# A fused attention-and-MLP kernel: the order of loads, LayerNorm steps and first projections in its head

## The chip, the cores and the metric

The kernel runs on one core of one Trainium2 chip. The metric is device time in microseconds (us) of one execution, lower is better. TensorE multiplies matrices, VectorE (DVE) and ScalarE (ACT) work on elements and empty the accumulators, GpSimd (POOL) works on elements in SBUF, and SyncE (SP) issues most transfers. ACT issues some transfers too, on a DMA queue of its own.

## What is computed

```python
xn = layernorm(x)                                   # x: 2048 x 448, bf16
qkv = xn @ wqkv                                     # 448 x 1344, 16 heads of 28
pq, pk = q @ w_phi[h], k @ w_phi[h]                 # per head 28 x 28
phi = concat(softmax(p), softmax(-p))               # for q and for k: 56 features a head
kv, z = phi_k^T @ v, sum(phi_k)                     # per head 56 x 28, and 56
o = (phi_q @ kv) / (phi_q @ z + 1e-6)
out = x + o @ wo + silu(xn @ w1) @ w2               # w1: 448 x 1792, w2: 1792 x 448
```

All sums over the sequence are linear, so `kv` and `z` are accumulated over all 2048 rows first, and the outputs are made in a last phase.

## The kernel before

**Tiling.** The 2048 rows are 16 tiles of 128 rows (`t`), in four chunks of four tiles (`c`). The depth of 448 is seven slices of 64 rows (`s`). Operands lie twice, in partitions 0 to 63 (LO) and 64 to 127 (HI), and matmuls are issued in pairs (`pair`, L420; all matmuls carry L429, all transposes by TensorE L442), one on each half of the array. Three double banks of PSUM, the slots, are handed round by `take` and `give`; a slot can be written again when its last content has been copied out.

**The units of work.** `LN_a` and `LN_b` (L529 to L548) make the LayerNorm of one tile: on DVE statistics (`bn_stats`, L532, 128x448), `bn_aggr` (L533), the variance plus epsilon (L535, on DVE for tiles 0 and 1, else on POOL), on POOL the power -0.5 (L537), and on DVE the normalised tile `xnd` (L547). Tiles 0 to 3 are transposed by TensorE (`X_tr`), and `X_ev` (L570) copies the two halves to `xT`, one with ACT (L447) and one with DVE (L579). Tiles 4 to 15 are transposed by DMA (`X_dma`, L559). `F1` is `xn @ w1` for one `i` of seven (128 columns of each half of `w1`) and two or four tiles, followed by Silu on ACT into `hT`; `F1p` is the same for one tile and two `i`. `FT_tr` transposes the q and k part of `wqkv`, and its four or three results are copied out by ACT and DVE (L768); `FM` multiplies them with the block-diagonal `BD` of `w_phi` into `wqk`, and each of the four FM results is copied out half by ACT and half by DVE (L788). `QK` is `xn @ wqk` for a tile, with two Exp on ACT, sums on DVE (L620), a reciprocal (L622) and two products on POOL (L627). `V` is `xn @ wv` for two tiles. `F2_early` is `hT @ w2` for one tile (28 matmuls). `KV` accumulates `kv` and `z`.

**What sets the order.** The program is recorded as a list of operations with dependencies, and a planner (`_Prog.schedule`, L199) decides the order on each engine. TensorE's operations stay in the order in which they are written down. Operations with `ordered=True` keep their written order among themselves on their engine; all loads are ordered. The others are sorted by the planner with costs that stand in the code; a transfer is taken to cost `nbytes / 280` ns after those before it (L300). Each engine then works strictly in its planned order and waits on semaphores.

**The head.** The loads are issued on SP as: x tile 0, x tile 1, `w1` part 0 and part 1, x tiles 2-3, `w1` part 2 and 3, wqk (two loads), `w_phi` (four small loads into `BD`), x tiles 4-7, `wv` (two loads), then `w2` in two loads, each after a mark in TensorE's order. `w1` has four parts of 256, 256, 256 and 128 columns; each part is a low load on SP (L493) and a high load on ACT's queue (L494). TensorE's order is: 36 warm-up pairs; `X_tr` of tile 0; 3 warm-up pairs; `X_tr` of tile 1; 3 warm-up pairs; `F1p` of tile 0 and of tile 1; `F1` for `i` 2 to 6 of tiles 0 and 1, with `X_tr` of tiles 2 and 3 between; `F1` for all seven `i` of tiles 2 and 3 with `FT_tr` (two) and `FM` 0 and 1 between; then `phase_e(0)` (L851): V(0), FM(2), F2_early(0) with FM(3) in its middle, QK(0), QK(1), F2_early(1), QK(2), QK(3), V(2). After that the four-tile `F1` of chunk 1 begins.

DVE's order in the head (what the planner made of it) is: statistics of tiles 0 and 1, `xnd` of tile 0 and the first part of tile 1, the copy of tile 0, the rest of `xnd` of tile 1, **`bn_stats` of tile 2, then the copy of tile 1**, the rest of tiles 2 and 3, their copies, and then `bn_stats` of tile 4 ahead of the first `FT_tr` copies.

Of the kernel before, what the change touches and what calls it, by code (L numbers as in the profile page):

```python
# [138 lines left out]
class _Prog:  # L139
# [89 lines left out]
    def _pass(self, when):  # L229
        ops = self.ops  # L230
        n = len(ops)
        lat = self.lat
        tend = max(when.values()) + 3000.0
        for o in reversed(ops):
            if o.eng == "pe":
                o.alap = when[o.id]
                continue
            m = tend
            for u in o.users:
                uu = ops[u]  # L240
                if u in o.odeps:
                    continue
                m = min(m, uu.alap - (lat(o, uu) if o.id in uu.deps else 0.0))
            extra = 0.0
            if o.is_dma:
                extra = o.fixed if o.fixed is not None else 2000.0 + o.nbytes / 280.0
            o.alap = m - o.dur - extra
# [24 lines left out]
        while done < n:  # L272
            best = None
            for e in ENGINES:
                if not ready[e]:
                    continue
                c = [(est(ops[i]), ops[i]) for i in ready[e]]
                t0 = min(x[0] for x in c)
                t, o = min(((t, o) for t, o in c if t <= t0 + WAIT_TOL), key=lambda x: (x[1].alap, x[1].id))
                for t2, o2 in c:  # L280
                    if o2 is o or o2.alap >= o.alap or t2 >= t + o.dur:
                        continue
                    la = max(t - o.alap, t + o.dur - o2.alap, 0.0)
                    lb = max(t2 - o2.alap, t2 + o2.dur - o.alap, 0.0)
                    if lb < la - 1.0:
                        t, o = t2, o2
                if best is None or t < best[0]:
                    best = (t, o)
            assert best is not None, "scheduler deadlock"
            t, o = best  # L290
            ready[o.eng].discard(o.id)
            o.start = t
            if o.is_dma:
                issue_end = t + o.dur
                eng_free[o.eng] = issue_end
                if o.fixed is not None:
                    o.end = t + o.fixed
                else:
                    x0 = max(issue_end + 900.0, dma_free[0])
                    dma_free[0] = x0 + o.nbytes / 280.0  # L300
                    o.end = dma_free[0] + 300.0
            else:
                o.end = t + o.dur
                eng_free[o.eng] = o.end + (0.0 if o.eng == "pe" else 30.0)
                if o.eng == "act" and o.table is not None:
                    act_table[0] = o.table
            order[o.eng].append(o.id)
            done += 1
            for u in o.users:
                ndeps[u] -= 1  # L310
                if ndeps[u] == 0:
                    ready[ops[u].eng].add(u)
# [3 lines left out]
def bass_parallel_sum__linear_kernel_hedgehog__dense_activation_silu__prompt_kernel(  # L316
# [16 lines left out]
    NB = 4  # L333
# [4 lines left out]
    with es:  # L338
# [117 lines left out]
        def load(dst, src, nbytes, name, eng="sp", issue=650.0, after=None):  # L456
            return P.dma(lambda e: e.dma_start(out=dst, in_=src), nbytes, writes=[dst], name=name, eng=eng,  # L457
                         issue=issue, ordered=True, after=after)
# [5 lines left out]
        pool(lambda e: e.memset(neghalf[:], -0.5), 110, [], [neghalf[:]], "neghalf")  # L464
        pool(lambda e: e.memset(ones_bf[:], 1.0), 230, [], [ones_bf[:]], "ones")
        pool(lambda e: e.affine_select(ident[:], ones_bf[:], [[1, 128]], ALU.is_equal, 0.0, base=0,
                                       channel_multiplier=-1), 290, [ones_bf[:]], [ident[:]], "ident")
# [16 lines left out]
        def load_x(t0, t1, after=None):  # L484
            load(x_sb[:, t0:t1, :], xv[:, t0:t1, :], (t1 - t0) * 128 * D * 2, f"x{t0}", issue=430, after=after)

        w1v = B_w1.rearrange("(s p) f -> p s f", p=64)
        W1S = [0, 256, 512, 768, 896]

        def load_w1(i):  # L490
            a, b = W1S[i], W1S[i + 1]
            n = D * (b - a) * 2
            load(w1_sb[LO, :, a:b], w1v[:, :, a:b], n, f"w1l{i}")  # L493
            load(w1_sb[HI, :, a:b], w1v[:, :, 896 + a:896 + b], n, f"w1h{i}", eng="act")  # L494
# [3 lines left out]
        load_w1(0)  # L498
        load_w1(1)
        load_x(2, 4)  # L500
        load_w1(2)
        load_w1(3)
        load(wraw[:, 0:3, 8:904], A_wqkv[0:384, 0:896].rearrange("(b p) c -> p b c", p=128), 384 * 896 * 2, "wqk0")
        load(wraw[LO, 3, 8:904], A_wqkv[384:448, 0:896], 64 * 896 * 2, "wqk1")
        pool(lambda e: e.memset(BD[:], 0.0), 300, [], [BD[:]], "bd0")
        for p0 in (0, 904):
            pool(lambda e, p0=p0: e.memset(wraw[:, :, p0:p0 + 8], 0.0), 150, [], [wraw[:, :, p0:p0 + 8]], "wpad")
        wpv = A_w_phi.rearrange("(k q l) d f -> q l d k f", q=2, l=2)
        for q in range(2):
            for l in range(2):  # L510
                p0 = (64 if q else 8) + l * DH
                load(BD[p0:p0 + DH, :, l * DH:(l + 1) * DH], wpv[q, l], DH * NB * DH * 2, f"wphi{q}{l}", issue=430)
        wvv = A_wqkv[:, 2 * D:3 * D].rearrange("(s p) c -> p s c", p=64)
        load_x(4, 8)
        load(wv_sb[LO], wvv, D * D * 2, "wv0")
        load(wv_sb[HI], wvv, D * D * 2, "wv1")
# [4 lines left out]
        for sl in range(NE):  # L521
            pads = E[:, sl].rearrange("p k (c n) -> p (k c) n", n=64)[:, :, 56:64]
            pool(lambda e, pads=pads: e.memset(pads, 0.0), 330, [], [pads], "pads")
        for sl in range(NV):
            onesc = vb[:, sl].rearrange("p t (h c) -> p (t h) c", c=DH + 1)[:, :, DH:DH + 1]
            pool(lambda e, onesc=onesc: e.memset(onesc, 1.0), 150, [], [onesc], "vones")


        def LN_a(t, od=False):  # L529
            P.unit = f"LN{t}"  # L530
            xs = x_sb[:, t, :]
            P.op("dve", 630, lambda e: e.bn_stats(st6[:, t, :], xs), [xs], [st6[:, t, :]], name="bnst", ordered=od)  # L532
            P.op("dve", 180, lambda e: e.bn_aggr(mv[:, t, :], st6[:, t, :]), [st6[:, t, :]], [mv[:, t, :]], name="bnag", ordered=od)  # L533
            P.op("dve" if od else "pool", 90 if od else 220,
# [15 lines left out]
        def LN(t):  # L550
            LN_a(t)
            LN_b(t)
# [17 lines left out]
        def X_ev(t, sl, od=False):  # L570
            P.unit = f"X{t}"
            j = t % 4
            for q in range(2):
# [19 lines left out]
        def F1p(t, i):  # L593
            P.unit = f"F1p_{t}_{i}"
            sl = take()
            for u in range(2):
                for s in range(NS):
                    pair([(bank(2 * sl + q)[:, u * 128:(u + 1) * 128], w1_sb[HALF[q], s, (i + u) * 128:(i + u + 1) * 128],
                           xT[HALF[q], 0, s, t * 128:(t + 1) * 128], s == 0, s == NS - 1) for q in range(2)], 128, "f1")
            src = two(sl)[:, :, 0:256].rearrange("p b (u n) -> p b u n", u=2)  # L600
# [30 lines left out]
        def V(t):  # L631
# [3 lines left out]
            for s in range(NS):  # L635
                pair([(bank(2 * sl + q)[:, 0:D], xT[HALF[q], c % NXC, s, (j + q) * 128:(j + q + 1) * 128], wv_sb[HALF[q], s, :],
                       s == 0, s == NS - 1) for q in range(2)], D, "v")
            dstv = vb[:, (t // 2) % NV].rearrange("p t (h c) -> p t h c", c=DH + 1)[:, :, :, 0:DH]
# [88 lines left out]
        def WO(t, ub, sl):  # L727
# [19 lines left out]
            P.dma(lambda e: e.dma_start(out=ov[:, t:t + 2, :], in_=x_sb[:, t:t + 2, :]), 2 * 128 * D * 2,  # L747
# [45 lines left out]
        LN_a(0, True)  # L793
        LN_a(1, True)
        PARTS = ((0, HS), (HS, NS))
        LN_b(0, PARTS, True)
# [5 lines left out]
        X_ev(0, s0, True)  # L802
        LN_b(1, PARTS[1:], True)
        P.unit = "warm"
        warm(3)
        X_tr(1, s1, 0, HS)
        X_tr(1, s1, HS, NS)
        X_ev(1, s1, True)
        P.unit = "warm"
        warm(3)  # L810
        give(s0)
        F1p(0, 0)
        give(s1)
        F1p(1, 0)
        for t in (2, 3):
            LN_a(t)
            LN_b(t)
        marks = []
        for i in range(2, FH):
            F1(0, i, 0, 2)  # L820
            marks.append(P.ops[P.last[("pe", "o")]])
            if i in (3, 5):
                t = 2 + (i - 3) // 2
                sl = take()
                X_tr(t, sl, 0, NS)
                X_ev(t, sl)
                give(sl)
        for i in range(FH):
            F1(0, i, 2, 2)
            marks.append(P.ops[P.last[("pe", "o")]])  # L830
            if i in (0, 2):
                FT_tr(i // 2)
            if i in (4, 6):
                FM((i - 4) // 2)
        load(w2_sb[:, 0:7], w2v[:, 0:7], FF * D, "w2", after=marks[5])
        load(w2_sb[:, 7:14], w2v[:, 7:14], FF * D, "w2", after=marks[6])

# [13 lines left out]
        def phase_e(c, f2):  # L851
            t = 4 * c
            if c == 0:
                V(0)
                FM(2)
                F2_early(f2[0], lambda: FM(3))
                QK(0)
                mk = P.ops[P.last[("pe", "o")]]
                load_x(8, 12, after=mk)
                load_x(12, 16, after=mk)  # L860
                QK(1)
                F2_early(f2[1])
                QK(2)
                QK(3)
                V(2)
# [4 lines left out]
            if c == 1:  # L870
                for s in range(NS):
                    for q in range(2):
                        load(wo_sb[HALF[q], s, :], wov[s], 64 * D * 2, f"wo{s}", after=mk)
# [148 lines left out]
```

## Time and profile before

| | us |
|---|---|
| median of 6 runs (157.48 to 158.63) | 157.72 |
| the profiled execution | 157.05 |
| its span, first to last instruction | 155.3 |
| TensorE busy | 145.7 (94%) |
| DVE / ACT / POOL busy | 93.9 / 93.4 / 84.0 |
| mean granted TensorE clock | 0.989 |
| start of the first V matmuls | 25.05 |
| start of the first QK matmuls | 30.03 |
| start of chunk 1's `F1` matmuls | 39.30 |

Times in the profile count from the span's first instruction. In the timeline a line gives the start, the length from the first to the last instruction of a merged group, the engine, the source line, the operation, output and input, the count, and in brackets how long the engine had been idle and who ended it. The waits list sums such idle time. The chain of waits follows what ended last back to the start. The stretches give busy time of each engine with the number of instructions, the granted clock, the DMA engines' busy share and GB/s. "To landing" is the time from the start of a transfer's issue to its last byte's report.

### The profile page before, as it was taken

What the parts mean: (1) busy time and instruction counts of PE and PEld (TensorE: products, weight loads), DVE (VectorE), ACT (ScalarE), POOL (GpSimd) and SP (SyncE); (2) the same over time, 40 slices, a digit from 0 to 9 for tenths busy, and PEclk for the clock granted to TensorE, in tenths of its full rate; (3) what the DMA queues carried; (4) which work ended last, traced back from release to release, by engine and by line L of the source; (5) the groups of instructions that cost most, each with busy time, mean ns of one, the idle gap of its engine ahead of it and who ended that gap; (6) DMA issues with size and microseconds to landing.
All of it is one profiled execution on the core that took longest, in us unless ns stands there. A gap on an engine that the chain in (4) does not pass through costs nothing.

```text
span 155.3 us, 5241 instructions
## 1 busy us (share of the span) xinstructions
PE 145.7 (94%) x2290; PEld 95.5 (61%) x2290; DVE 93.9 (60%) x170; ACT 93.4 (60%) x120; POOL 84.0 (54%) x97
## 2 busy tenths in 40 slices
PE   5829998999999999999999999999999999999990
PEld 5729887666556666555666666666556666666650
DVE  2744197639996667990129797862046464946652
ACT  3215788597995977795689577588563324033330
POOL 6412007022899995969902999977993311222220
PEclk9995999999999999999999999999999999999999
DMA  4999987783030895397883022523170020111203
GB/s 120 236 241 299 174 257 207 125 195 124 0 72 4 160 181 121 93 90 148 163 153 59 4 68 68 72 68 72 41 166 2 4 103 19 63 59 56 72 0 118
DMA packets 38639, 16.60 MB, mean 107 GB/s; under 512 B 30104, under 2 KB 38232, under 8 KB 38616
## 3 DMA queue, kind: packets, MB, share of 16 engines
q1 hardware_dynamic: 36760, 15.47, 45.7%
q10 hardware_dynamic: 1856, 0.80, 2.4%
q8 instruction: 18, 0.29, 0.9%
q14 instruction: 5, 0.04, 0.1%
HBM read 7.48 MB, written 1.84 MB: 60 GB/s over the span
## 4 chain that ended last, share of the span: by engine, by line
PE 89%; DMA 4%; SPq 1%; DVE 1%; issue 1%; ACT 1%; DVEq 0%
PE psum L429 87%; DMA x_sb<-in_A_x_dram 4%; PE psum L442 2%; SPq L457 1%; DVE st L532 0%; DVE x_sb L743 0%; ACT hT L447 0%; DVEq L973 0%; ACT xT L447 0%; DVE xT L579 0%; DVE mv L533 0%
## 5 line engine op out<-in xcount | busy, mean ns | idle before, releaser
L627 POOL TENSOR_TENSOR E<-E,Rk 128x896 bf16<-128x896 bf16 x32 | 53.2, 1697 | 10.1 <-DVE Rk L622 8.3
L429 PE MATMUL psum<-xT,w_sb 64*128 64x512 bf16 (+2 forms) x518 | 48.0, 332 | 2.9 <-DVE mv L533 2.7
L429 PE MATMUL psum<-w_sb,hT 64*128 64x448 bf16 x448 | 45.4, 349 | 0.0
L447 ACT ACTIVATE hT<-psum 128x1024 bf16<-128x1024 f32 (+1 forms) x35 | 29.2, 853 | 13.9 <-PE psum L429 13.2
L429 PEld LDWEIGHTS psum<-xT,w_sb 64*128 64x128 bf16 x518 | 27.3, 97 | 16.0 <-issue 2.9
L620 DVE TENSOR_REDUCE Sk<-E 128x64 f32<-128x1792 bf16 x16 | 31.9, 2003 | 5.1 <-ACT E L447 4.9
L429 PEld LDWEIGHTS psum<-w_sb,hT 64*128 64x128 bf16 x448 | 25.2, 94 | 15.4
L447 ACT ACTIVATE E<-psum 128x896 bf16<-128x896 f32 x32 | 27.4, 917 | 6.6 <-PE psum L429 5.2
L447 ACT ACTIVATE xT<-psum 128x896 bf16<-128x896 bf16 (+2 forms) x20 | 13.0, 690 | 27.7 <-PE psum L442 25.4
L429 PE MATMUL psum<-wqk,xT 64*128 64x448 bf16 x224 | 23.7, 349 | 0.0
L689 POOL TENSOR_TENSOR xT<-xT,x_sb 128x448 f32<-128x448 f32 x8 | 8.3, 1034 | 25.1 <-ACT xT L447 22.4
L429 PEld LDWEIGHTS psum<-wqk,xT 64*128 64x128 bf16 x224 | 13.0, 94 | 7.8
L547 DVE TENSOR_SCALAR xnd<-x_sb,mv,rstd 128x896 bf16<-128x896 bf16 (+2 forms) x18 | 11.5, 666 | 8.7 <-POOL rstd L537 8.6
L677 POOL TENSOR_TENSOR Ye<-Ye,x_sb 128x448 f32<-128x448 f32 x8 | 8.2, 1031 | 12.9 <-DVE Ye L675 12.9
L532 DVE BATCH_NORM_STATS2 st<-x_sb 128x6 f32<-128x448 bf16 x16 | 9.4, 606 | 7.8 <-DMA x_sb<-in_A_x_dram 7.8
L429 PE MATMUL psum<-wv_sb,xT 64*128 64x448 bf16 x112 | 12.1, 349 | 0.0
L429 PE MATMUL psum<-wo_sb,xT 64*128 64x448 bf16 x112 | 11.9, 349 | 0.0
L535 POOL TENSOR_SCALAR ve<-mv 128x1 f32<-128x1 f32 x14 | 2.8, 216 | 15.9 <-DVE mv L533 15.9
L675 DVE TENSOR_TENSOR Ye<-psum,Ye 128x448 f32<-128x448 f32 x8 | 5.0, 621 | 9.2 <-ACT Ye L447 6.0
L714 DVE TENSOR_TENSOR xT<-psum,rden 128x224 bf16<-128x224 f32 x32 | 10.2, 381 | 0.2
L537 POOL TENSOR_TENSOR rstd<-ve,neghalf 128x1 f32<-128x1 f32 x16 | 8.9, 565 | 1.7 <-DVE ve L535 1.0
L743 DVE TENSOR_TENSOR x_sb<-psum,Ye 128x448 bf16<-128x448 f32 x8 | 4.6, 619 | 7.7 <-PE psum L429 7.7
(45 smaller groups left out, 112.5 us busy)
## 6 DMA issues: line engine op xcount, KB each, us to landing
out_dram<-x_sb SPq DMA_DIRECT2D x8, 224.0 KB, 1.9
w_sb<-in_B_w_dram SPq DMA_DIRECT2D x2, 784.0 KB, 5.5
x_sb<-in_A_x_dram SPq DMA_DIRECT2D x3, 448.0 KB, 4.4
wv_sb<-in_A_wqkv_dram SPq DMA_DIRECT2D x2, 392.0 KB, 10.2
wo_sb<-in_A_wo_dram SPq DMA_DIRECT2D x14, 56.0 KB, 2.2
w_sb<-in_B_w_dram ACTq DMA_DIRECT2D x3, 224.0 KB, 5.2
w_sb<-in_B_w_dram SPq DMA_DIRECT2D x3, 224.0 KB, 6.1
phT<-in_A_wqkv_dram SPq DMA_DIRECT2D x1, 672.0 KB, 10.8
```

What stands on the lines that cost most here:

```text
L429: ins = e.matmul(dst, lhsT, rhs, start=st, stop=sp, skip_group_check=True)
L447: return P.op("act", d_act(n), lambda e: e.activation(dst, src, func, scale=scale), reads=reads or [src], writes=writes or [dst], table=ta ...
L532: P.op("dve", 630, lambda e: e.bn_stats(st6[:, t, :], xs), [xs], [st6[:, t, :]], name="bnst", ordered=od)
L537: P.op("pool", 580, lambda e: e.tensor_tensor(rstd[:, t:t + 1], ve[:, t:t + 1], neghalf[:], ALU.pow), [ve[:, t:t + 1], neghalf[:]], [rstd[ ...
L547: lambda e, dst=dst, src=src: e.tensor_scalar(dst, src, mv[:, t, 0:1], rstd[:, t:t + 1], ALU.subtract, ALU.mult),
L620: dve(lambda e: e.tensor_reduce(Sk[:, t % 3, :].rearrange("p (h g) -> p h g", g=2), Er, AXL.X, ALU.add), d_dve(1792), [Er], [Sk[:, t % 3, ...
L627: pool(lambda e, Eh=Eh, Rb=Rb: e.tensor_tensor(Eh, Eh, Rb, ALU.mult), 1770, [Eh, Rh], [Eh], "phi%d" % qk)
L675: dve(lambda e: e.tensor_tensor(y, b, y, ALU.add), d_dve(D), [b, y], [y], "ye_d")
L677: pool(lambda e: e.tensor_tensor(y, y, x_sb[:, t, :], ALU.add), 1110, [y, x_sb[:, t, :]], [y], "ye_x")
L689: pool(lambda e: e.tensor_tensor(y, y, x_sb[:, t, :], ALU.add), 1110, [y, x_sb[:, t, :]], [y], "yl_x")
L714: dve(lambda e, dst=dst, src=src, rb=rb: e.tensor_tensor(dst, src, rb, ALU.mult), d_dve(224), [src, r], [dst], "o")
L743: dve(lambda e, b=b, y=y, dst=dst: e.tensor_tensor(dst, b, y, ALU.add), d_dve(D), [b, y], [dst], "out")
```

## The change

It does the following.

- The loads: `w1` comes in three parts of 256, 256 and 384 columns. x tiles 2-3 are issued after `w1` part 0 instead of after part 1. The four `w_phi` loads go to ACT's queue, after its three `w1` loads. x tiles 4-7 become two loads of two tiles, no longer ahead of `wv`: SP's order after wqk is `wv`, x 4-5 (after the mark of `F1` i=3, tiles 0-1), the first half of `w2` (after i=5), x 6-7 (after i=5), the second half of `w2` (after i=6). The loads of x tiles 8-15 stand ahead of the four transposing DMAs of tiles 4-7 on SP; before they stood behind them.
- POOL: the constants and the clearing of `BD` and of the pads of `wqk`'s raw tile are ordered, the first constants ahead of `BD`; the nine other memsets (`pads`, `vones`) come after the powers of tile 3.
- DVE and POOL run tiles 0 to 3 in a written order. `bn_stats` of tile 2 still stands ahead of the copy of tile 1. The epsilon step of tiles 2 and 3 goes from POOL to DVE.
- TensorE: ten warm-up pairs stand after `X_tr` of tile 0 (instead of three and three); `X_tr` of tile 1 comes in the middle of `F1p` of tile 0; `X_tr` of tile 3 and the `FT_tr` and `FM` steps move by one `F1` or two; `phase_e(0)` is V(0) with FM(2) inside, V(2) with FM(3) inside, QK(0), QK(1), F2_early(0), QK(2), QK(3), F2_early(1).
- The planner's cost of a transfer is `nbytes / run * (12 + 0.0475 * run) / 16` ns, with `run` the bytes of one contiguous piece. With it the planner puts all four DVE copies of the `FT_tr` results together; then come `bn_stats` of tiles 4 and 5, the copies of FM(0) and FM(1), `bn_stats` of tile 6, the copy of FM(2), `bn_stats` of tile 7, the copy of FM(3), and then the four `bn_aggr` and the four `xnd` of tiles 4 to 7. Before, the four `xnd` stood between the copies of FM, and all four `bn_stats` ahead of them.

From chunk 1's `F1` on, the order of TensorE's units is the same as before.

```diff
-        W1S = [0, 256, 512, 768, 896]
+        W1S = [0, 256, 512, 896]
...
         load_w1(0)
+        load_x(2, 4)
         load_w1(1)
-        load_x(2, 4)
         load_w1(2)
-        load_w1(3)
...
-                load(BD[...], wpv[q, l], DH * NB * DH * 2, f"wphi{q}{l}", issue=430)
+                load(BD[...], wpv[q, l], DH * NB * DH * 2, DH * 2, f"wphi{q}{l}", eng="act", issue=430)
...
-        load_x(4, 8)
...
-        LN_a(0, True)
-        LN_a(1, True)
         PARTS = ((0, HS), (HS, NS))
+        LN_st(0, True)
+        LN_ag(0, True)
+        LN_st(1, True)
+        LN_ag(1, True)
...
-        X_ev(0, s0, True)
+        X_ev(0, s0, (0, 1), True)
         LN_b(1, PARTS[1:], True)
+        LN_st(2, True)
         P.unit = "warm"
-        warm(3)
-        X_tr(1, s1, 0, HS)
-        X_tr(1, s1, HS, NS)
-        X_ev(1, s1, True)
-        P.unit = "warm"
-        warm(3)
+        warm(10)
         give(s0)
-        F1p(0, 0)
+
+        def x1():
+            X_tr(1, s1, 0, HS)
+            X_tr(1, s1, HS, NS)
+            X_ev(1, s1, (0, 1), True)
+            LN_ag(2, True)
+            LN_st(3, True)
+            LN_ag(3, True)
+            LN_b(2, od=True)
+            LN_b(3, od=True)
+            pads_init()
+
+        F1p(0, 0, x1)
         give(s1)
         F1p(1, 0)
-        for t in (2, 3):
-            LN_a(t)
-            LN_b(t)
...
-            if i in (3, 5):
+            if i in (3, 4):
...
-            if i in (0, 2):
+            if i in (1, 3):
                 FT_tr(i // 2)
-            if i in (4, 6):
-                FM((i - 4) // 2)
-        load(w2_sb[:, 0:7], w2v[:, 0:7], FF * D, "w2", after=marks[5])
-        load(w2_sb[:, 7:14], w2v[:, 7:14], FF * D, "w2", after=marks[6])
+            if i in (5, 6):
+                FM(i - 5)
+        load_x(4, 6, after=marks[1])
+        load(w2_sb[:, 0:7], w2v[:, 0:7], FF * D, 896, "w2", after=marks[3])
+        load_x(6, 8, after=marks[3])
+        load(w2_sb[:, 7:14], w2v[:, 7:14], FF * D, 896, "w2", after=marks[4])
...
-                V(0)
-                FM(2)
-                F2_early(f2[0], lambda: FM(3))
+                V(0, lambda: FM(2))
+                V(2, lambda: FM(3))
                 QK(0)
                 mk = P.ops[P.last[("pe", "o")]]
+                QK(1)
+                F2_early(f2[0])
                 load_x(8, 12, after=mk)
                 load_x(12, 16, after=mk)
-                QK(1)
-                F2_early(f2[1])
                 QK(2)
                 QK(3)
-                V(2)
+                F2_early(f2[1])
```

`LN_st` and `LN_ag` are the first and the other steps of `LN_a`; `F1p` and `V` call what they are given after the first of their two halves and after their third slice.

## The prediction, made before the result was known

> **What bounds the kernel now.** I read the waits of TensorE first, then the chain, then the timeline of the head, then the stretches with the clock. The chain ends in one TensorE piece without a gap:
>
> ```profile
> 3.15 6.59 DMA x_sb<-in_A_x_dram
> ...
> 9.76 0.63 DVE st L532
> 10.39 0.29 DVE xT L579
> ...
> 10.83 3.78 PE psum L429 x56
> ...
> 27.13 87.45 PE psum L429 x1114
> ```
>
> From 27.13 to 114.58 nothing but TensorE is on the path, and little else to the end. So the change can win only before 27.13, and whatever it wins there moves the end one for one, as long as TensorE finds its operands at chunk 1 (39.30 now). TensorE's waits up to there:
>
> ```profile
> PE psum L429 <- DVE mv L533: 2.7, 1, 2.7
> PE psum L429 <- POOL ident L466: 1.7, 1, 1.7
> PE psum L429 <- issue: 0.5, 1, 0.5
> PE psum L442 <- DVE xnd L547: 0.4, 1, 0.4
> ```
>
> The longest one is named after DVE's L533, but DVE's timeline shows what it is:
>
> ```profile
> 9.76 0.63 DVE L532 BATCH_NORM_STATS2 st<-x_sb 128x6 f32<-128x448 bf16 x1 [2.94 <-DMA x_sb<-in_A_x_dram]
> 10.30 0.37 DVE L579 COPY xT<-psum 128x448 bf16<-128x448 bf16 x1
> ...
> 19.36 0.63 DVE L532 BATCH_NORM_STATS2 st<-x_sb 128x6 f32<-128x448 bf16 x1 [1.94 <-DMA x_sb<-in_A_x_dram]
> 19.91 0.74 DVE L768 COPY phT<-psum 128x512 bf16<-128x512 bf16 x2
> ```
>
> The copy of tile 1, which TensorE needs for F1p(1), stands behind bn_stats of tile 2, which waits for x 2-3. The same pattern comes again at 19.36: bn_stats of tile 4 waits for x 4-7 and holds the FT copies. The idle time also costs clock:
>
> ```profile
> 8.40:11.80 3.40, 0.97 (x32) 1.00 (x34) 1.73 (x6) 0.33 (x1) 0.86 (x3) 1.00 1.23 236
> 11.80:15.20 3.40, 3.40 (x47) 3.02 (x45) 1.63 (x3) 1.75 (x4) 0.70 (x2) 0.51 1.06 302
> ```
>
> After a stretch in which TensorE was busy 0.97 of 3.40 us the clock is 0.51 for as long: 3.4 x 0.49 = 1.7 us of work lost. DMA is at 1.06 to 1.23 throughout: the head is fed by a saturated queue.
>
> **The loads in the new order.** Issue plus time to landing gives, in us, x0 2.9, x1 3.4, w1 low parts 6.4, 8.6, 11.6, 12.3, high parts 4.9, 7.0, 10.1, 10.7, x 2-3 9.7, wqk 15.9 and 16.8, x 4-7 19.3, wv 20.1 and 21.2, w2 23.3 and 26.5. I move these steps as a queue.
>
> - x 2-3 take 1.17 (9.74 - 8.57) behind w1 part 0, no longer behind part 1: 6.4 + 1.2 = 7.6. w1 part 1 then ends where both ended before, 9.75.
> - w1's last two parts took 2.6 (9.74 to 12.34). Their 688 KB moved at about 240 GB/s with 512-byte pieces and 215 with 256-byte ones, 2.98 us; the piece of 768 bytes is not in the trace. Bounds: no gain, and 1.0 at the 359 GB/s of 12 to 13 us (1792-byte pieces). I take 0.7, nearest to the 512-byte row. The four w_phi loads now share the engines with this part: 24 KB in 448 pieces, 0 to 0.56 us if a piece costs as much as those of the transposes (800 a us at 28 us); I take 0.3. So w1 is complete at 12.34 - 0.7 + 0.3 = **11.9**.
> - wqk follows 4.5 later as now: 16.4. From there to the end of wv were 4.3, of which x 4-7 (448 KB at 255 to 310 GB/s) were 1.6: wv at 19.1. x 4-5 follow 0.8 later, 19.9; the first w2 half at 340 GB/s, 2.2; x 6-7, 0.7: **22.8**. Check: what lies ahead of and in x 6-7 is the very set that had landed at 23.25 before, with the queue nearly dry (72 GB/s) from 18.4 to 20.4.
>
> The DMA page of the Trainium skill (DMA: Bandwidth & Descriptors, section Queues, rings and completion order) says that an engine takes turns between the queues by packet, which speaks against putting w_phi beside w1's last part; an estimate by it would delay that part by up to w_phi's whole time. No row separates the two.
>
> **TensorE step by step.** F1p(1) starts 1.09 after x 2-3 land now (9.74 to 10.83: bn_stats 0.63, copy 0.37). New: 7.6 + 1.1 = 8.7, **instead of 10.83**. Ahead of it all fits: ten warm-up pairs are 0.5 (three are 0.16), ending near 6.5, when ACT's copy of tile 0 (5.96 + 0.54) ends too. F1p(1) ends at 9.5, F1(2) waits for w1 part 1 to 9.8, two F1 (0.77 each; 28 matmuls took 1.54) and X_tr(2) (0.2) end at 11.55, and F1(4) waits for w1's last part: 11.9. So half of what x 2-3 win is lost to w1, a queue that the move doesn't shorten.
>
> From 11.9: ten F1 7.7, X_tr 0.2, two FT 0.92, two FM 0.44 give V(0) at 21.2; three of its seven pairs (0.57), FM(2) 0.22, the rest 0.76, three pairs of V(2) 0.57: FM(3) at 23.3. Its slot was FM(2)'s, whose DVE copy now stands behind bn_stats of tile 6: 22.8 + 0.63 + 0.62 (L788) + 0.1 = 24.15, a **new wait of 0.85**. (At FM(0) the same pattern with x 4-5 at 19.9 costs 0.5, which the later wait swallows.) Queued behind FM(3) are V(2)'s rest and QK(0): 24.15 + 0.15 + 0.76 = 25.05. Four QK and two F2 (1.325 and 2.65 each) end at 35.65, where chunk 1's F1 starts, **instead of 39.30: 3.65 less**. In this I let no clock drop remain, since the new idle pieces (0.9, 0.3, 0.35, 0.85) lie apart.
>
> What hides the rest: the nine POOL memsets moved (six of 0.3, three of 0.24, 2.6 in all) lie at 10.4 to 13, and POOL is next needed after x 4-7, beyond 24. The epsilon step on DVE is 0.15 instead of POOL's 0.22. The w_phi issues take 1.9 (6.33 to 8.23 on SP) and end on ACT near 5.3, 0.6 ahead of its first copy; if longer, the wait for w1 still covers a us. ident comes 0.2 earlier and moves only warm-up work. Exp starts with a table load (1.28) behind V(2)'s copy; the two Exp of QK(0) then end near 29.1, and QK(2), which wants that slot, comes at 30.4. Transposes of tiles 4 to 7 now stand behind x 8-15 on SP: issued from QK(0)'s end plus about 1.1, at 1.3 each, landing 3.0 after the last issue, some 9.4 after QK(0)'s start; if they also queue behind 896 KB at 340 to 390 GB/s, 10.2 to 10.7; needed at 10.6. I charge 0.15. Sum: 3.5 less.
>
> The Trainium skill (TensorE: Matmul & The Clock Gate, section Why this matters for your kernels) wants no idle gaps over about 3 us; here 2.74 us cost 3.4 us at half clock, so the trace is stricter. If the rule held, the drop would have another cause and could stay: the sum by it would be 1.8 less, not 3.5.
>
> **Rivals.**
>
> 1. x 6-7 land by 21.9 and the copies never wait: TensorE runs through from 11.9, QK(0) at 24.2, chunk 1 at 34.8, 4.5 less: 153.2. For: the dry queue of 18.4 to 20.4. Against: the slowest engine reported wv only at 21.2. Chance 0.20.
> 2. The clock still drops: 1.7 back, 155.9. For: 0.97 busy of 3.40 sufficed. Against: the new gaps are short. 0.09.
> 3. tiles 4 to 7 land late behind x 8-15 and F1 of chunk 1 waits about 1: 155.2. 0.08.
> 4. Slower: x 6-7 behind wv and half of w2 hold FM(2)'s copy, FM(3) and QK(0) one for one. It decides from a landing at 22.8 + 3.65 = 26.4 on; at 27.4 the kernel is 1 us slower, 158.7. For: the second half of w2 landed at 26.5, and bn_stats of tile 4 did hold FT copies. Against: the bytes. 0.06.
> 5. x 2-3 don't land earlier, since ACT's queue takes the time that part 1 leaves (at 4 to 10 us both queues were full): F1p(1) at 10.8 and all behind it as before: 157.7. 0.05.
>
> **Numbers.** The profiled execution took 157.05 (span 155.3, 1.75 around it), 0.67 below the median 157.72. 157.05 - 3.5 = 153.55; on the scale of the median **154.2**, chance 0.52. The range 152.9 to 156.2 takes in rivals 1, 2 and 3 and the landing of x 6-7 from 21.5 to 24.6. About 0.5% (0.8 us) is what a measurement can tell from no change. Faster by more: 0.52 + 0.20 + 0.09 + 0.08 = 0.89; within: 0.05; slower: 0.06.
>
> **What would show it.** x 2-3 landing near 7.6 and F1p(1) near 8.7; clock 1.00 at 9 to 16 us; F1(4) waiting for DMA to 11.9; bn_stats of tile 6 with idle time from DMA ahead of it, and TensorE waiting at FM(3); QK(0) near 25 and chunk 1's F1 near 35.7. I am wrong if TensorE's waits move to ACT, if a stretch at 0.5 stays, or if idle time comes after 39.

## The result and the profile after

The changed kernel takes **158.86 us** (median of 27 runs, 157.83 to 160.86) against 157.75 (62 runs, 156.06 to 159.18) of the kernel before: ratio 1.008, 95% interval 1.006 to 1.010. It is slower by 0.8%, where 154.2 was forecast. The profiled execution took 158.86, its span is 157.1, the mean granted clock 0.978. Ratios below are all to the kernel before, on the same chip. A ratio leaves out executions more than 1.5% above the fastest of the same kernel; this weighs most in e2 below, where six of twelve fall out and the median of all twelve, 157.12, is 0.995 of the 157.89 of before.

The chain of waits of the changed kernel (start, length, what):

```profile
1.70 6.93 DMA w_sb<-in_B_w_dram
...
10.76 4.46 PE psum L429 x48
...
15.54 0.49 issue
...
21.25 0.42 issue
...
26.64 0.42 issue
...
36.63 4.58 DMA xT<-xnd
...
41.35 18.66 PE psum L429 x236
```

Chunk 1's F1 starts at 41.35, not at 39.30 as before and not at 35.65 as forecast. Three things stand on the chain: a load of `w1` near its head (before, one of x), three stops that no semaphore explains ("issue"; before, two of 0.20 and 0.47), and, wholly new, a transposing DMA ahead of chunk 1. TensorE's waits of the same profile name the same (total, times, longest):

```profile
PE psum L429 <- issue: 1.3, 3, 0.5
PE psum L442 <- DVE xnd L554: 1.2, 1, 1.2
PE psum L429 <- DMA xT<-xnd: 1.2, 1, 1.2
PE psum L429 <- DMA w_sb<-in_B_w_dram: 1.2, 1, 1.2
```

The old wait of 2.7 on F1p(1)'s copy is gone as such, but F1p(1) starts at 10.76 (before 10.83). DVE's timeline of the changed kernel shows why:

```profile
9.79 0.63 DVE L536 BATCH_NORM_STATS2 st<-x_sb 128x6 f32<-128x448 bf16 x1 [2.03 <-DMA x_sb<-in_A_x_dram]
10.33 0.37 DVE L587 COPY xT<-psum 128x448 bf16<-128x448 bf16 x1
```

It is the old pattern at the old time: x 2-3 land at 9.77 (before 9.74), and the copy of tile 1 stands behind their statistics. Ahead of it stand two waits of 1.2, one on `xnd` (0.4 before; x 1 lands at 4.84, before 3.44) and a new one on `w1` part 0 (8.62, before 6.41).

The stretches of the changed kernel (busy time with instructions for PE, PEld, DVE, ACT and POOL, then clock, DMA share, GB/s):

```profile
8.00:11.30 3.30, 2.58 (x54) 2.33 (x56) 1.48 (x5) 1.08 (x2) 0.24 (x1) 0.50 1.20 219
11.30:14.70 3.40, 3.40 (x45) 2.78 (x43) 1.93 (x5) 1.25 (x3) 2.84 (x11) 0.50 1.10 264
```

The half clock, one stretch before, is two now. **The account:** TensorE's named waits ahead of chunk 1 sum to 5.7 before and 6.3 after (with the wait for `ident`, 1.7 and 1.4), 0.6 more. Busy time at half clock cost 3.40 x 0.49 = 1.7 before and (2.58 + 3.40) x 0.50 = 3.0 after, 1.3 more. Together 1.9 of the 2.05 by which chunk 1 came later. This adds up one execution and shows no cause, and the clock's part is not borne out by the others: of the 25 executions counted, the twelve with a mean clock of 0.973 to 0.978, like the profiled one, took 158.66 on average, and the ten with 0.985 to 0.988, so with less time at half clock, took 159.18. The experiment a3 shows why it can be so. The profiled execution before lay 0.7 below its median, so the medians differ by less, 1.1. From chunk 1's F1 to the last matmul all seventeen profiles of this study show 111.8 to 112.0: only the head matters.

### The profile page after: what moved, and what is told of

Same layout as the page of the kernel before. It is cut to its first block, busy times and chain, and to the rows that moved or that the text cites. A ratio compares the mean times of both kernels' runs of the same rounds, so it can differ in the third digit from the quotient of the medians.

```text
span 157.1 us, 5256 instructions
## 1 busy us (share of the span) xinstructions
PE 147.0 (94%) x2298; PEld 93.6 (60%) x2298; DVE 94.0 (60%) x172; ACT 93.6 (60%) x120; POOL 83.7 (53%) x95
## 4 chain that ended last, share of the span: by engine, by line
PE 88%; DMA 7%; issue 1%; DVE 1%; SPq 1%; DVEq 0%
PE psum L429 86%; DMA w_sb<-in_B_w_dram 4%; DMA xT<-xnd 3%; PE psum L442 2%; SPq L460 1%; DVE Ye L687 0%; DVE x_sb L755 0%; DVEq L990 0%; SPq L567 0%
## 5 line engine op out<-in xcount | busy, mean ns | idle before, releaser
L429 PE MATMUL psum<-xT,w_sb 64*128 64x512 bf16 (+2 forms) x518 | 49.5, 340 | 3.4 <-DMA xT<-xnd 1.2
L429 PEld LDWEIGHTS psum<-w_sb,hT 64*128 64x128 bf16 x448 | 24.6, 94 | 16.5
L429 PEld LDWEIGHTS psum<-wqk,xT 64*128 64x128 bf16 x224 | 12.1, 94 | 8.6
L429 PE MATMUL psum<-wo_sb,xT 64*128 64x448 bf16 x112 | 11.9, 349 | 0.0
```

The source lines that it names most:

```text
L429: ins = e.matmul(dst, lhsT, rhs, start=st, stop=sp, skip_group_check=True)
```

## The experiments

The theories: ScalarE's queue, which starts 0.21 earlier in the changed kernel (first `w1` load at 0.93 instead of 1.14), delays x 1 and `w1` part 0 (in expectations A); the loads of x 8-15 ahead of the transposes delay chunk 1 (B); `w_phi` on ScalarE's queue slows the last part of `w1` (C); the wait and the half clock at F1p(1) are on the path (D); TensorE stops where its next block of instructions has not been fetched (F); a wait taken away at F1p(1) comes back at a later copy behind later statistics (E).

**a1_act_later: ScalarE's loads 0.21 later** (the changed kernel with `BD`'s memset ahead of POOL's constants, which shifts these loads back to 1.14).

```diff
+        P.op("pool", 300, lambda e: e.memset(BD[:], 0.0), [], [BD[:]], name="bd0", ordered=True)
...
-        P.op("pool", 300, lambda e: e.memset(BD[:], 0.0), [], [BD[:]], name="bd0", ordered=True)
```

> The changed kernel with one edit: POOL clears BD ahead of the first constant again, so that ACT's first load is issued some 0.2 us later, at about 1.14 as before the change (0.93 now). Theory A (the early start of ACT's queue puts w1's high parts ahead of x 1 and of w1's low part): x 1 lands near 3.5 instead of 4.84, w1's low part 0 near 6.5 to 7 instead of 8.62, x 2-3 near 8 instead of 9.77, the first F1p starts near 7.2; the total goes down by 0.3 to 1, the rest being held by w1's last part (13.85). Rival (the two queues share the engines by chance): landings within 0.5 of the changed kernel's, total the same.

Measured: 158.41, ratio 1.0024 (0.9999 to 1.005). x 1 lands at 3.99 (changed kernel 4.84), `w1` part 0 at 6.74 (8.62), F1p(0) starts at 7.00 (8.67), F1p(1) at 10.04. Five profiles with the early start show x 1 at 4.8 or later and F1p(0) at 7.8 to 9.3; those with the late start have F1p(0) at 6.9 to 7.4. That start is a cause, shown. But x 2-3 come at 8.95 even so, not at 7.6, and of 1.7 us gained at F1p(0) only 0.6 reach chunk 1 (40.74): two stops of 1.19 and 1.25 without a named cause follow, and the wait ahead of chunk 1 is 1.5.

**a2_x8_late: x 8-15 behind the transposes** (the changed kernel; the mark of these loads goes from QK(0) to QK(2)).

```diff
                 QK(0)
-                mk = P.ops[P.last[("pe", "o")]]
                 QK(1)
                 F2_early(f2[0])
+                QK(2)
+                mk = P.ops[P.last[("pe", "o")]]
                 load_x(8, 12, after=mk)
                 load_x(12, 16, after=mk)
-                QK(2)
```

> The changed kernel with one edit: the loads of x 8-15 take their mark from QK(2) instead of QK(0), which puts them behind the four transposing DMAs of tiles 4-7 on SP, as they stood before the change. Theory B (the transposes wait behind 896 KB on the queue and chunk 1's F1 waits for them): the wait of 1.2 us ahead of chunk 1's F1 (start 41.35) goes, F1 starts near 40.0, total 1.2 to 1.4 less than the changed kernel, 157.5, level with before. Rival (the transposes are late since their xnd are late, which stay behind all FM copies on DVE): the last transpose lands at 40 to 41 still, total within 0.5 of the changed kernel.

Measured: 157.78, ratio 1.0004 (0.997 to 1.0037), 1.2 us less than the changed kernel. Its chain runs into chunk 1 without a DMA:

```profile
29.92 10.21 PE psum L429 x108
40.13 0.06 issue
40.20 4.91 PE psum L429 x43
```

Chunk 1 starts at 40.20 instead of 41.35: the whole wait of 1.2. In all five profiles with x 8-15 ahead of the transposes this wait is there, 0.5 to 1.5; in the six with them behind it is 0.3 once (f2) and else nothing.

**a3_wphi_sp: `w_phi` back on SP, behind wqk** (the changed kernel).

```diff
-                load(BD[...], wpv[q, l], ..., eng="act", issue=430)
+                load(BD[...], wpv[q, l], ..., eng="sp", issue=430)
```

> The changed kernel with one edit: the four w_phi loads go back to SP's queue, behind wqk. Theory C (their 448 small pieces on ACT's queue slow w1's last low part): that part lands at 12.5 to 13 instead of 13.85, wqk and wv follow some 0.5 to 1 earlier, total 0.3 to 1 less. Rival (the part is late because everything ahead of it is): it lands within 0.5 of 13.85, total the same.

Measured: 158.58, ratio 1.0041 (1.0009 to 1.0074). `w1`'s last low part lands at 12.83 instead of 13.85. That sharing with `w_phi` cost it this 1.0 is not shown: in the nine profiles with `w_phi` on ScalarE's queue the part lands at 12.61 (c1) to 14.02 (f2), and in c2, with `w_phi` on SP, at 13.39. TensorE doesn't get the gain:

```profile
13.69 0.27 PE L429 MATMUL psum<-xT,w_sb 64*128 64x256 bf16 x2
16.09 0.99 PE L429 MATMUL psum<-xT,w_sb 64*128 64x256 bf16 x12 [2.12 <-issue]
```

Here the listed clock is 1.00 from 9.80 to 16.62, and F1(4) begins at 13.69, 1.6 before the changed kernel's 15.25. After its first pair TensorE stands still until 16.09, where the changed kernel's stop had ended too (16.03). So in these two profiles the half clock ahead of this stop has no price: the stop takes up what a full clock wins.

**a5_act_x8: a1 and a2 together** (both diffs above).

> The changed kernel with the edits of a1 and a2 together. If the two causes are independent (0.45 and 1.1 less alone), 157.3. By the fetch theory F (TensorE stands still where its 252-instruction blocks begin, at its instructions 441, 693 and 943, until a block of 16 KB has come through the loaded DMA engines) the two stops of 1.2 us that a1 showed at instructions 441 and 693 stay, and the transposes no longer hold chunk 1.

Measured: 157.42, ratio 0.9945 (0.9916 to 0.9974). Taken from 1.008, a1 gives 0.0056, a2 0.0076, both 0.0135: the two add up within their intervals of some 0.003 to either side, and without them the change would be a gain of 0.9 us. Its waits:

```profile
PE psum L429 <- issue: 2.4, 2, 2.2
...
PE psum L429 <- DVE mv L540: 1.2, 1, 1.2
```

F1p(1) starts at 9.40, the earliest of the changed kernel and its narrow variants, and the stop is the longest: 2.18, ending at 15.63.

**b2_stats_behind: the kernel before with statistics of tiles 2 and 3 behind tile 1's copy.**

```diff
-            LN_a(t)
-            LN_b(t)
+            LN_a(t, True)
+            LN_b(t, od=True)
```

> The kernel before the change with one edit: the LayerNorm of tiles 2 and 3 runs in the written order on DVE, behind the copy of tile 1 (its epsilon step then is on DVE too). Theory D (the wait of 2.7 us at F1p of tile 1 and the half clock after it are on the path): F1p of tile 1 starts near 7.9 instead of 10.83, no half clock, total 2 to 4 less. Rival E (what is won there is lost again at the next gate: x 4-7 land at 19.3, bn_stats of tiles 4 and 5 stand ahead of the FT copies, and FT of the second half waits for its slot until about 21.3 as before): chunk 1's F1 at 39 to 39.8, total within 0.5 of before.

Measured: 157.45, ratio 0.9961 (0.9928 to 0.9993). Its profiled execution took 158.99, 1.5 above the median, so only the kind of its waits is read, not their lengths:

```profile
PE psum L442 <- DVE xnd L547: 2.6, 2, 2.2
PE psum L442 <- DVE phT L768: 2.0, 1, 2.0
```

F1p(1) follows F1p(0) at once, and the wait goes on to the transposes of tile 2 and to the FT copies behind `bn_stats` of tile 4. E is seen; how much it takes back this profile can't tell.

**c1_wide: a5 with the warm-up pairs four times as wide and fewer** (11 of 512 columns for 46 of 128: about the same work in 140 TensorE instructions less, loads of weights counted).

```diff
-                pair([(bank(2 * sl + q)[:, 0:128], ident[HALF[q], :], ident[HALF[q], :], True, True) for q in range(2)],
-                     128, "warm", dur=d)
+                pair([(bank(2 * sl + q)[:, 0:512], ident[HALF[q], :],
+                       ident[HALF[q], None, :].broadcast_to([64, 4, 128]), True, True) for q in range(2)], 512, "warm", dur=d)
...
-        warm(32, d=107.0)
-        warm(4)
+        warm(8, d=428.0)
+        warm(1)
...
-        warm(10)
+        warm(2)
```

> a5 with one edit more: the 46 warm-up pairs of 128 columns become 11 pairs of 512 columns, the same TensorE time with 140 fewer instructions (weight loads and matmuls). Theory F: the block borders move 140 instructions on in the work, the stops move with them (from the F1 of i=4 to some 140 instructions later) or go, since the blocks are asked for when the work is further on; the sum of stops marked as waiting for nothing falls from some 2.4 us to under 1, total 0.5 to 1.5 less than a5. Rival (the stops belong to places of the work: a slot, a semaphore): they stay ahead of the same matmuls, total as a5.

Measured: 157.50, ratio 0.9969 (0.9933 to 1.0004): no gain on a5. The stop of 2.18 that ended at 15.63 is gone, but one of 0.19 ending at 17.79 and one of 1.44 ending at 24.21 stand later in the work. Counted in matmuls and weight loads, they fall on numbers 438 and 689; in the changed kernel and its narrow variants on 441, 693 and 943. So a stop belongs here to the number of an instruction, not to what it does.

**c2_wide_all: c1 with `w_phi` on SP (a3's diff) and the statistics of tile 2 behind the copy of tile 1.**

```diff
-        LN_st(2, True)
...
             X_ev(1, s1, (0, 1), True)
+            LN_st(2, True)
```

> c1 with w_phi back on SP's queue and bn_stats of tile 2 behind the copy of tile 1 (the planner then puts bn_stats of tiles 4 and 5 between the FT copies on DVE again). If theories A, B, C, D and F all hold, F1p of tile 1 starts near 8 to 8.5, F1 of i=4 near 12.5 to 13 when w1's last part lands, total 155.5 to 156.3, under before. Rival (the loads set the pace whatever TensorE does: wqk at 17, wv at 20): within 0.5 of c1.

Measured: 157.65, ratio 0.9969 (0.9937 to 1.0001). F1p(1) starts at 8.52, and F1(2) stands 1.86 until 11.34, listed as "issue" too, but `w1` part 1 landed just before, at 11.24; then stops of 0.67 and 1.72 follow. The two further edits bring nothing together with c1.

**d1_before_wide: the kernel before with wide warm-ups alone** (11 pairs for 42).

```diff
-        warm(32, d=107.0)
-        warm(4)
+        warm(8, d=428.0)
+        warm(1)
...
-        warm(3)
+        warm(1)
...
-        warm(3)
+        warm(1)
```

> The kernel before the change with one edit: 42 warm-up pairs of 128 columns become 11 of 512 columns. Theory F: its two stops that wait for nothing (0.2 at instruction 693, 0.47 at 944) go or move, total 0.3 to 0.7 less than before, and the long wait for tile 1's copy (2.7) stays. Rival: same stops, same total.

Measured: 157.14, ratio 0.9939 (0.9904 to 0.9974). The stop of 0.47 that ended at 27.13 before is gone, chunk 1 starts at 38.60 (39.30), though the wait on F1p(1)'s copy is 3.1 there (2.7).

**e1_no_warm: the kernel before without warm-ups** (it leaves out these multiplications, whose results are not used).

```diff
-        warm(32, d=107.0)
-        warm(4)
...
-        warm(3)
...
-        warm(3)
```

> The kernel before (with its order of loads), without any of the warm-up multiplications ahead of and between the head's first steps (they compute nothing that is used). It separates the half clock from the instruction blocks as the price of the head. The block theory: 196 TensorE instructions fewer than in the kernel before, so no stop without a named cause in the head; a half clock that lies over stretches in which TensorE waits for loads costs little; total within 0.5 us of 157.14 (the kernel before with wide warm-ups), chunk 1 at 38.3 to 39.0 against 38.60. The clock theory: without warm-ups the head up to 11 runs at half clock and one window more follows; F1(2), F1(4) and what stands behind them come 1.5 to 3 us later; total 158.5 to 160.

Measured: 157.10, ratio 0.9944 (0.9914 to 0.9975), the same as d1. A stretch of its profile:

```profile
11.30:14.70 3.40, 3.24 (x46) 2.92 (x48) 2.27 (x6) 0.63 (x2) 1.56 (x4) 1.00 1.12 263
```

46 matmuls take 3.24 us, as slow as the 45 in 3.40 at clock 0.50 in the changed kernel, though 1.00 is listed; the record of the clock begins only at 16.4 here. The 28 matmuls of F1p(0), from 6.96 on, took 1.68, before 0.94. So TensorE ran at half speed up to 16.4. In the profile chunk 1 came 0.9 later than in d1 (39.51, past what either theory had given for it), in the medians nothing shows. The clock theory's 158.5 to 160 is ruled out; a price of up to some 0.7, by the two intervals, is not. As e1 has 44 matmuls and weight loads less than d1 too (168 less than before, not 196), part of a price could hide behind these.

**e2_w2_late: c1 with x 6-7 right behind x 4-5, and `w2` behind multiplications of tiles 2 and 3.**

```diff
             F1(0, i, 2, 2)
+            marks.append(P.ops[P.last[("pe", "o")]])
...
-        load(w2_sb[:, 0:7], w2v[:, 0:7], FF * D, 896, "w2", after=marks[3])
-        load_x(6, 8, after=marks[3])
-        load(w2_sb[:, 7:14], w2v[:, 7:14], FF * D, 896, "w2", after=marks[4])
+        load_x(6, 8, after=marks[1])
+        load(w2_sb[:, 0:7], w2v[:, 0:7], FF * D, 896, "w2", after=marks[8])
+        load(w2_sb[:, 7:14], w2v[:, 7:14], FF * D, 896, "w2", after=marks[10])
```

> The changed kernel with ScalarE's loads later, x 8 to 15 behind the transposes and wide warm-ups, and with w2's halves moved behind x 6-7 and behind multiplications of tiles 2 and 3, so that the load queue is empty earlier. The block theory in its queue form (the stop is long because the block's transfer takes turns with loads): the stop of 1.44 before matmul 689 falls below 0.7, x 6-7 land 2 us earlier, QK(0) at 27.4 to 28.2 instead of 28.45, total 156.2 to 157.0 instead of 157.50. Rival: the stop belongs to the block alone and stays at 1.2 or more; total 157.2 to 157.8. Third: w2 comes late for F2 and its wait appears in TensorE's waits; total 158 or more.

Measured: 157.12 (154.65 to 159.24), ratio **0.9867** (0.9828 to 0.9905), 155.8 on the scale of before. The profiled execution took 155.73; whether the longest of the twelve have stops no trace shows. TensorE's waits of the whole profile have no stop left:

```profile
PE psum L429 <- POOL ident L470: 1.7, 1, 1.7
PE psum L429 <- DVE mv L540: 1.4, 1, 1.4
PE psum L429 <- ACT hT L447: 0.8, 1, 0.8
PE psum L429 <- ACT xT L447: 0.7, 1, 0.7
```

QK(0) starts at 27.44 (c1 28.45), chunk 1 at 38.04 (39.04). The DMA view of 18.3 to 22.9 us, first c1, then e2 (packets, MB and mean rate; then the load queue's share of 16 engines):

```profile
DMA packets 1731, 1.67 MB, mean 362 GB/s; under 512 B 44, under 2 KB 1730, under 8 KB 1730
...
q1 hardware_dynamic: 1730, 1.65, 106.7%
```

```profile
DMA packets 430, 0.57 MB, mean 124 GB/s; under 512 B 40, under 2 KB 429, under 8 KB 429
...
q1 hardware_dynamic: 429, 0.56, 58.9%
```

In these stretches lies one packet of the instruction queue each, 16 KB: in c1 from 21.69 to 22.80, with TensorE standing until 24.21; in e2 from 20.52 to 21.59, 1.6 ahead of the matmul that needs it, which runs on.

**e3_wide_stats: d1 and b2's edit** (both diffs above).

> The kernel before with wide warm-ups and with tiles 2 and 3's statistics put behind tile 1's copy of F1p: the two edits that gained most alone. Order theory (the wait of 3.15 on F1p(1)'s copy is the head's price): the two gains add up, 157.1 less 0.3 to 0.8, so 156.3 to 156.8. Rival (the wait only moves: tiles 2 and 3's normalisation, now later, and the copies behind later statistics take it up again): 157.0 to 157.4, with waits of about 2 us on xnd and phT.

Measured: **155.61** (155.22 to 156.01), ratio 0.9851 (0.9827 to 0.9875), the best of this study; more than the expected 156.3 to 156.8, and more than the product of the two single ratios, 0.990. F1p(1) starts at 8.19, chunk 1 at 37.85. Its waits:

```profile
PE psum L442 <- DVE xnd L547: 2.4, 2, 2.2
PE psum L429 <- POOL ident L466: 1.7, 1, 1.7
```

The wait on `xnd` of tile 2 takes the place of the 3.1 on the copy, but the one on FT's copies, 2.0 in b2, is gone. Whether the wide pairs took it away or b2's long execution had made it stays open.

**e4_after_wide: the changed kernel with wide warm-ups alone** (c1's diff).

> The changed kernel with wide warm-ups alone: 140 TensorE instructions fewer ahead of the first block's end, everything else as in the change. The block theory: the three stops of 0.49, 0.42 and 0.42 shift to later matmuls and come to less than 0.6 together, total 0.4 to 0.9 below the changed kernel, about 158.0 to 158.5; the wait of 1.2 on the transposed x before chunk 1 stays. Rival (the head is set by the loads and the half clock alone): total within 0.2 of the changed kernel's 158.86.

Measured: 158.43, ratio 1.0034 (1.0012 to 1.0057). The total is in the range of the block theory; the view is not: the three stops became one of 2.0 ending at 19.33, and the wait ahead of chunk 1 fell to 0.5 as TensorE came there later.

**f1_w2_late: the changed kernel with e2's order of loads alone** (e2's diff).

> The changed kernel with nothing else altered than x 6-7 right behind x 4-5 and w2's halves behind multiplications of tiles 2 and 3 on SP (narrow warm-ups, ScalarE's loads early, x 8 to 15 ahead of the transposes). Queue theory (a block's fetch takes turns with the loads): with w2 away the second and third stop of 0.42 each go, the first (at 16.03, while wv still lands) stays; QK(0) at 28.4 to 28.9 instead of 29.39, total 0.4 to 1.0 below the changed kernel, 157.9 to 158.5. Rival, count theory (a stop belongs to how many instructions a block holds): the three stops stay, total within 0.2 of 158.86. The wait on the transposed x before chunk 1 may stay or grow, since x 8 to 15 land no later than before.

Measured: 159.33 (157.47 to 160.70), ratio 1.0048 (1.0004 to 1.0093). The third stop is gone, the second stays at 0.42, the first grows from 0.49 to 0.97: neither theory as put, and no difference from the changed kernel that can be told.

**f2_act_x8_w2: e2 with the narrow warm-ups of the changed kernel** (a1, a2 and e2's diffs, without c1's).

> As the run with w2 behind multiplications of tiles 2 and 3 and wide warm-ups (ratio 0.987), but with the narrow warm-ups of the changed kernel: 140 more TensorE instructions ahead of the first border. Queue theory: the stop at matmul 441 stays near 2 (it lies at 15 to 16, when wqk and wv are still landing, and w2's place doesn't touch it), the one at 693 goes; total about 1 above the wide form, 156.6 to 157.2. Count theory: both stops stay, 157.3 to 157.8. If the stops are no matter at all, the total is that of the wide form, 155.8.

Measured: 158.10, ratio 1.0007 (0.997 to 1.0044), 1.4% above e2 by the ratios and 0.6% by the medians of all executions, with only 46 small pairs in place of 11 wide ones between them. Its waits:

```profile
PE psum L429 <- issue: 2.6, 2, 1.3
...
PE psum L429 <- DVE mv L540: 1.6, 1, 1.6
...
PE psum L429 <- DMA xT<-xnd: 0.3, 1, 0.3
```

The stops of 1.34 and 1.23 are there again, 2.57 together, and chunk 1 starts 2.54 later than in e2 (40.58). In these two profiles the stops make up the difference, and the instruction count decides on them. That the move of `w2` alone shortens them is refuted by f1 and f2: f2 is a5 with `w2` later, and it is slower than a5 (0.9945). It takes both edits, since c1, wide with `w2` early, has stops of 1.6.

**f3_best: e3 with `w2` later.**

```diff
-        load(w2_sb[:, 0:7], w2v[:, 0:7], FF * D, "w2", after=marks[5])
-        load(w2_sb[:, 7:14], w2v[:, 7:14], FF * D, "w2", after=marks[6])
+        load(w2_sb[:, 0:7], w2v[:, 0:7], FF * D, "w2", after=marks[8])
+        load(w2_sb[:, 7:14], w2v[:, 7:14], FF * D, "w2", after=marks[10])
```

> The kernel before with wide warm-ups, tiles 2 and 3's statistics behind tile 1's copy, and w2's halves behind multiplications of tiles 2 and 3. In the same kernel with w2 where it was, no stop without a named cause is left; queue theory then expects nothing more from w2's move: 155.4 to 155.8, against 155.61. Rival: w2 also slows the x loads and weights of that stretch, and its move brings a further 0.5 to 1: 154.6 to 155.1.

Measured: 158.67, ratio 1.0036 (0.9999 to 1.0073). Neither expectation: in the order of before, F2_early comes ahead of QK(0), and its weights are late now.

```profile
PE psum L429 <- DMA w_sb<-in_B_w_dram: 2.4, 1, 2.4
```

So the move paid in e2 alone (against c1), where F2_early stands behind QK(1) and the warm-ups are wide.

## Why the prediction was wrong

Chunk 1 came at 41.35 instead of 35.65. Of these 5.7 us, 3.35 were lost up to F1(4) (15.25 instead of 11.9), 1.0 from there to QK(0) (29.39 instead of 25.05), and 1.35 from QK(0) to chunk 1.

1. **"6.4 + 1.2 = 7.6"** for x 2-3 behind `w1` part 0. The first step that failed, in its first term: part 0 came at 8.62 instead of 6.4, because ScalarE's queue began 0.21 earlier. With the early start it lands at 7.25 to 9.29, with the late one at 5.91 to 6.74 in the kernels with the changed order. Behind it x 2-3 took 1.15, as forecast, and landed at 9.77. But where part 0 is early they take 2.2 to 3.1 behind it, so 8.31 (a5) is the best that was seen. That ScalarE's `w1` loads beside them take that time is argued, not shown. Rival 5, with a chance of 0.05, had F1p(1) at 10.8, and 10.76 came, by luck: its reason, that ACT's queue takes the time that part 1 leaves, is not what happened here, and its "all behind it as before" was too good.
2. **"w1 is complete at ... 11.9"**. It was 13.85, and 12.61 to 14.02 in the other kernels with the changed order. Which term was too small stays open; that the charge of 0.3 for `w_phi` was is not shown (a3). The rule of the Trainium skill that the prediction names, that an engine takes turns between the queues by packet (DMA: Bandwidth & Descriptors, section Queues, rings and completion order), is neither borne out nor refuted by these landings. In the changed kernel F1(4) did not wait for this part: with F1p(1) at 10.76 and the half clock, TensorE was busy until 15.22, as the chain's 4.46 from 10.76 shows.
3. **"I let no clock drop remain"**. There were two half-clock stretches instead of one, 1.3 us of busy time by the account. The two waits of 1.2, on `xnd` and on `w1` part 0, were not in the sum, and with them TensorE was busy 1.66 of the 3.41 from 4.52 to 7.93, ahead of the drop. Its price does not show in the total (the 25 executions, a3, e1). That waits for loads and blocks take it up is seen in a3 and argued for the rest.
4. **"ten F1 7.7, X_tr 0.2, two FT 0.92, two FM 0.44 give V(0) at 21.2"**. A sum of busy times with no stops. The waits of before had "issue: 0.5", which the prediction showed and did not carry on. In the seven kernels with the changed order and narrow warm-ups (the changed kernel, a1, a2, a3, a5, f1, f2) TensorE begins its number 440 at 13.2 to 15.5, and number 441 comes at 14.8 to 16.3 behind a stop. It comes 1.35 to 1.57 after the end of a packet of the instruction queue, whether TensorE was there early (a5, 13.2, then 15.63) or late (a2, 15.5, then 16.13). So most of what is won ahead of that number is lost at it. (Before, that packet had ended 2.6 ahead of its use.) With the loads as forecast, F1(4) at 11.9 would likely have met the same stop; that was not tried.
5. **The wait of 0.85 at FM(3)** did not come; x 6-7 were late (24.05 against 22.8), but so was TensorE. (0.15 of that is the sum's own: 784 KB at its 340 GB/s take 2.36, not 2.2.)
6. **"I charge 0.15"** for the transposes behind x 8-15: 1.2, and a2 takes it back whole. The mechanism was named, as rival 3 too; the size was off by eight times.
7. Right were: the head alone decides, one for one (111.8 to 112.0 from chunk 1 on), and F1p(1)'s wait is the copy behind the statistics (e3).

Two of these are shown to have made the changed kernel slower than before: the early start of ScalarE's queue and x 8-15 ahead of the transposes (a5). What keeps a5 from the forecast is in part shown (the stops) and in part open (the landings of points 1 and 2). The new order itself is worth less than the 3.5 that was forecast. In e2, with points 1 and 6 undone and wide warm-ups, it stands 2.1 us below before by the ratio; but the wide pairs alone bring 1.0 of that (d1), and with the order of loads of before, wide pairs and one edit to the statistics bring 2.4 (e3).

## What to carry to other kernels

A sum of busy times in a head must also hold the stops listed as "issue": look whether they fall on the same instruction number, and count instructions as a cost; wide operations instead of many small ones moved them here, which alone gained some 0.5% in d1 and e4 and nothing in c1. Compare the landings of loads, not their positions in the order: here the start of one queue moved those of the other. What stood ahead of a transposing DMA on its queue was paid at the operation that needed the transpose. And compare several profiles before a landing is put down to one edit: the last part of `w1` landed up to 1.4 apart in the eleven kernels with the changed order.

## What the hardware showed that was not expected

- **Blocks of instructions.** The trace's instruction queue carries packets of 16 KB. In each of 23 stops of these profiles (one is listed under ACT) TensorE went on 1.25 to 1.58 us after such a packet's end, at numbers 250 to 253 apart in matmuls and weight loads. Four other pauses listed as "issue" end 0.1 after a part of `w1` landed instead. A packet takes 0.9 to 1.6. How long after the last border it starts varies from 0.4 to 5.4; what sets it is not settled. At the changed kernel's first stop the timeline has (idle time in brackets):

```profile
15.25 0.28 PE L429 MATMUL psum<-xT,w_sb 64*128 64x256 bf16 x2
16.03 0.83 PE L429 MATMUL psum<-xT,w_sb 64*128 64x256 bf16 x12 [0.49 <-issue]
```

  The packet before it ended at 14.65. The Trainium skill (Runtime: NRT & Kernel Launch, section Instruction fetch mechanics) says of a 16 KiB border that its cost is "mostly hidden"; the stops of up to 2.2 us here differ.
- **0.21 us of start.** A second queue that starts 0.21 earlier delayed the first queue's x 1 by 0.9 and `w1` part 0 by 1.9 (a1 against the changed kernel); over eleven profiles x 1 lands at 4.84 or later with the early start and at 4.07 or earlier with the late one.
- **A listed clock of 1.00** is no proof of full speed where the clock's record begins later, as in e1: the time of like matmuls tells it.
